# Attention beside a gated MLP: VectorE filler in measured portions, and the last output projection moved to the end

## The chip, the cores and the metric

The kernel runs on one core of a Trainium2 chip. The metric is the time of one execution on the device, in microseconds; the kernel before takes 751.76 us (median of three, 750.97 to 756.8). The engines of a core run side by side, each through its own queue of instructions in order, and meet through semaphores: TensorE (PE) multiplies matrices into PSUM, VectorE (DVE) adds and multiplies, ScalarE (ACT) copies and applies functions, GpSimd (POOL) and SyncE (SP) mostly start DMA transfers, as ScalarE can too.

## What is computed

```python
# A_x: 1 x 2048 x 1024 bf16; wqkv: 1024 x 3072; wo: 1024 x 1024
# w1, w3: 1024 x 3584; w2: 3584 x 1024
xn = layernorm(x)
qkv = (xn @ wqkv).reshape(B, S, 3, 32, 32)          # 32 heads of 32
idx = pos[:, None] - (arange(8) * 2)[None, :]       # 8 keys back, every 2nd
logits = einsum(q, k[idx]) * 32 ** -0.5             # idx < 0 masked
s = (softmax(logits) @ v[idx]).reshape(B, S, 1024) @ wo
h = silu(xn @ w1) * (xn @ w3)
g = silu(h @ w2)
out = x + s * g
```

Every token attends to 8 tokens (itself, and 2, 4, ... 14 back). There is no matrix product in the scores or the values: they are elementwise products of q, k and v with shifted views, on VectorE.

## The kernel before

**Products.** Each matrix product is done in blocks of 2 x 2 with seven products instead of eight. The function `seven` does one: with `a`, `b` for the two operands' quarters, `s` and `t` for sums of quarters, it runs the products a11 b11, s1 t1, a12 b21, (the product left over from the block before), s2 t2, s4 b22, s3 t3 on TensorE, eight 128x512 matmuls each, 56 in all. Between them ScalarE copies partial results from one PSUM tile to another (`act_copy`, L158), and VectorE adds the final combinations (`e12`, `e22`). PSUM has four tiles of 128x1024 f32, so a late copy or addition holds up a later product. The sums of weights (s, t) are made on VectorE, in the first half of the tokens, written out to `s_dram` and `t_dram`, and read back for the second.

**Stages.** Tokens fall in two halves b = 0, 1 of 1024, and attention in four chunks c = 0 to 3 of 512. The order of the matmuls is: layer norm and transposes, then six sevens for q, k and v (to about 170 us); `mlp_up(0)`, 14 blocks `fb` of 256 columns of w1 and w3 (170 to 350); `mlp_down(0)` (350 to 438); `wo(0)` (438 to 462); `mlp_up(1)` (462 to 637.5); `wo(1)` (637.5 to 664); `mlp_down(1)`, whose results `gated` multiplies with the attention output of `wo(1)` and adds to x (664 to the end).

**In a block of `mlp_up`** VectorE makes four sums of weights for the next block (`w_sums`, L547 to L550, 128x1024), the additions `um` (L581) and `h_sb` (L594) from PSUM and the product of the gate (L603, 128x2048). Every second block it also makes four sums of w2 (`w2_step`, L618 to L621, 128x1024). Their loads come through SyncE's queue into a ring of nine slots (`wring`, `r4`, `release`); a slot that is written out to DRAM can take a new load only when the write has landed.

**Attention as filler.** `scores` (L405 to L408: one product 128x4096 for each of 8 shifts, then three adds that halve), `score_sums` (sums over a head's 32 dimensions, on TensorE), `softmax` (L423 to L437) and `values` (L444 to L457) are VectorE work that fills the spaces between the sums. They are emitted in steps (`att_step`) with a low priority `BG`, at a few places of the stages, and the scheduler sets them into VectorE's order where it expects room; `behind(key)` keeps an instruction behind another on the same engine. `fetch_k` and `fetch_v` bring the next chunk through GpSimd's queue.

**`park`** gives a tile `pk` for a part of q, k or v that goes to DRAM, and a function `fin` that issues its write, on ScalarE's queue, together with one write of `spill` (the operands of the second half).

Of the kernel before, what the change touches and what calls it, by code (L numbers as in the profile page):

```python
# [17 lines left out]
def kernel(  # L18
# [161 lines left out]
    def seven(key, A, B, e11, e12, e22, e21, snap=None):  # L180
# [21 lines left out]
        act_copy(su2[:], pb[:])  # L202
        for i in I:
            mm(pe[:, i], s4[i], b22, False)
# [3 lines left out]
        e22(pb, sp5)  # L208

# [119 lines left out]
    def park(t, c, j0, name):  # L329
        tl = k4(name, (2, CH), BF16)  # L330
        dst = (q_dram, k_dram, v_dram)[t][c, :, j0:j0 + 2, :]

        def fin():
            m = nc.scalar.dma_start(out=dst, in_=tl[:])
            if spill:
                d, f = spill.pop(0)
                with tc.issue_after(m.ins):
                    nc.scalar.dma_start(out=d, in_=f)

        return tl[:], fin  # L340
# [6 lines left out]
    def qkv_copy(t, c, j0):  # L347
        def f(ps, *a):
            d, fin = qkv_dst(t, c, j0)
            with hp():  # L350
                if a:
                    nc.vector.tensor_add(d, ps[:], a[0][:])
                else:
                    anchor["c", t, c, j0] = nc.scalar.copy(out=d, in_=ps[:])  # L354
                fin()
        return f
# [29 lines left out]

    def fetch_k(c):
        if c == 0:
            return
        nc.gpsimd.tensor_copy(out=kT[:, :, 0:HALO], in_=kT[:, :, CH:CH + HALO])  # L390
# [4 lines left out]
    def fetch_v(c):  # L395
        nc.gpsimd.tensor_copy(out=vT[:, :, 0:HALO], in_=vT[:, :, CH:CH + HALO])
        nc.gpsimd.dma_start(out=vT[:, :, HALO:], in_=v_dram[c])

    def scores(c):
        q = qt[c]  # L400
        E = att_tile((W, CH), BF16, f"Es{c}")
        for w in range(W):
            o = HALO - DIL * w
            p_t = att_tile((NJ, CH), BF16, f"pt{c}_{w}")
            nc.vector.tensor_mul(p_t[:], q[:], kT[:, :, o:o + CH])  # L405
            nc.vector.tensor_add(p_t[:, 0:4, :], p_t[:, 0:4, :], p_t[:, 4:8, :])  # L406
            nc.vector.tensor_add(p_t[:, 0:2, :], p_t[:, 0:2, :], p_t[:, 2:4, :])
            nc.vector.tensor_add(E[:, w, :], p_t[:, 0, :], p_t[:, 1, :])  # L408
        sc[c] = E

    def score_sums(c):
        E = sc[c]
        zp = bank2(f"zp{c}")
        for h in range(2):
            for sq in range(4):
                nc.tensor.matmul(
                    zp[sq * 32:(sq + 1) * 32, h].rearrange("p (w t) -> p w t", t=P), lhsT=ones4[:],
                    rhs=E[:, h * 4:(h + 1) * 4, sq * P:(sq + 1) * P], start=True, stop=True,
                )
        sc[c] = E[:].bitcast(FP32).rearrange("p w n -> p (w n)").rearrange("p (a w t) -> p a w t", a=2, t=P)  # L420
        nc.scalar.copy(out=sc[c][:, 0], in_=zp[:].rearrange("p h (w t) -> p (h w) t", t=P))

    def softmax(c):  # L423
        Z = sc[c]
        z, zm, zs = Z[:, 0], Z[:, 1, 0:4], Z[:, 1, 4:8]
# [4 lines left out]
        nc.scalar.activation(out=z, in_=z, func=ACTF.Exp, scale=scale)  # L430
# [8 lines left out]
    def values(c, pairs=(0, 2, 4, 6)):  # L439
        E = pr[c]  # L440

        def pvmul(dst, w):
            o = HALO - DIL * w
            nc.vector.tensor_mul(dst, E[:, w, :].unsqueeze(1).to_broadcast([P, NJ, CH]), vT[:, :, o:o + CH])  # L444

        A = oT[:, c % 2]
        for w0 in pairs:
            B = att_tile((NJ, CH), BF16, f"B{c}_{w0}")
            if w0 == 0:
                pvmul(A, 0)  # L450
                pvmul(B[:], 1)
            else:
                C = att_tile((NJ, CH), BF16, f"C{c}_{w0}")
                pvmul(B[:], w0)
                pvmul(C[:], w0 + 1)
                nc.vector.tensor_add(B[:], B[:], C[:])
            nc.vector.tensor_add(A, A, B[:])  # L457

    def att_steps():
        with priority(BG - 10000):  # L460
            scores(0)
        yield
        score_sums(0)
        fetch_k(1)
        with priority(BG):
            softmax(0)
            scores(1)
            values(0)
            fetch_v(1)
        yield  # L470
        with priority(BG + 9000):
            fetch_k(2)
        yield
        score_sums(1)
        with priority(BG + 10000):
            softmax(1)
            scores(2)
            values(1)
            fetch_k(3)
            fetch_v(2)  # L480
        yield
        score_sums(2)
        with priority(BG + 20000):
            softmax(2)
        yield
        with priority(BG + 30000), behind("wo"):
            scores(3)
            values(2, (0, 2, 4))
        yield
        score_sums(3)  # L490
        with priority(BG + 40000):
            softmax(3)
            values(2, (6,))
            fetch_v(3)
            values(3)
        yield

    att_it = att_steps()

    def att_step():  # L500
        next(att_it)
# [17 lines left out]
    def up_load(b, fb):  # L519
# [7 lines left out]
        else:  # L527
            up_sums(b, fb, w1t, w3t)
            sa, s4 = tiles[b, fb][2:]
            nc.sync.dma_start(out=sa[:], in_=s_dram[fb, :, 0:2])  # L530
            nc.sync.dma_start(out=s4[:], in_=s_dram[fb, :, 3])
# [3 lines left out]
    def up_sums(b, fb, w1t, w3t):  # L535
        sa = r4(("sa", fb), (2, KH, 2 * P), FP16)
        half.append(half.pop(0))
        s4 = slot(5, (KH, 2 * P), FP16, half[0] * SLOT // 2)
        tiles[b, fb] = w1t, w3t, sa, s4

    def w_sums(fb):
        up_sums(0, fb, *tiles[0, fb])
# [3 lines left out]
        with behind(("m", fb - 1)):  # L546
            nc.vector.tensor_add(sa[:, 0], a21, a22)  # L547
            nc.vector.tensor_sub(sa[:, 1], sa[:, 0], a11)
            nc.vector.tensor_sub(s4[:], a12, sa[:, 1])
            nc.vector.tensor_sub(s3, a11, a21)  # L550
# [11 lines left out]
    def mlp_up(b, steps={}):  # L562
        order = [*range(b * FB // 2, FB - 1), *range(b * FB // 2), FB - 1]
        for n, fb in enumerate(order):
            steps.get(n, lambda: None)()
            if n == 0:
                up_load(b, fb)
                if b == 0:
                    w_sums(fb)
                up_load(b, order[1])  # L570
# [8 lines left out]
            def e12(pe, su2):  # L579
# [5 lines left out]
                if b == 0:  # L585
                    anchor["m", fb] = m
                    if fb + 1 < FB:
                        w_sums(fb + 1)
                if n + 2 < FB:
                    up_load(b, order[n + 2])  # L590

            def e22(pb, sp5):
                with hp():
                    m = nc.vector.tensor_add(h_sb[:, f2, CH:], pb[:], sp5[:])  # L594
                if b == 0:
                    anchor["t", fb] = m
                    w2_step(fb)

            def e21(pb, f2=f2, hl=hl, n=n, fb=fb):
                release(("w3", fb))  # L600
                with hp():
                    nc.scalar.copy(out=hl["g"][:, :, 0:CH], in_=pb[:])  # L602
                    nc.vector.tensor_mul(h_sb[:, f2, :], h_sb[:, f2, :], hl["g"][:])  # L603

            seven(f"m{b}_{fb}", up_A(b, fb), B0, e11, e12, e22, e21)

    def w2_step(fb):
        if fb % 2 == 0:
            tiles["t"] = [r4("t", (2, 2, CH)) for x in range(2)]
            for x in range(2):  # L610
                nc.sync.dma_start(out=tiles["t"][x][:], in_=w2_q[:, fb:fb + 2, x])
            return
        q = tiles["t"]
        q16 = [t[:].bitcast(FP16) for t in q]
        b11, b12, b21, b22 = [q[x][:, :, y] for x in range(2) for y in range(2)]
        o1, o3, o4, o2 = [q16[x][:, :, y] for x in range(2) for y in range(2)]
        with behind(("t", fb)):
            nc.vector.tensor_sub(o1, b12, b11)  # L618
            nc.vector.tensor_sub(o3, b22, b12)
            nc.vector.tensor_sub(o2, b22, o1)  # L620
            nc.vector.tensor_sub(o4, b21, o2)  # L621
        for x in range(2):
            nc.gpsimd.dma_start(out=t_dram[:, fb - 1:fb + 1, 2 * x:2 * x + 2], in_=q16[x])
        release("t")
# [13 lines left out]
    def mlp_down(b, done=lambda *a: None, mid=lambda n: None):  # L638
        NQ = (0, 4, 8, 11, 14)

        def rhs_tiles(kind, fh=0, dh=0, t=0):
            key = kind, fh, dh, t
            ops = [key]
            for f0, f1 in zip(NQ, NQ[1:]):
                wt = r4(key, (f1 - f0, CH), FP16 if kind == "t" else BF16)
                if kind == "t":
                    nc.sync.dma_start(out=wt[:], in_=t_dram[:, f0:f1, t, :])
# [23 lines left out]
        def sums(gp):  # L671
# [3 lines left out]
            with hp():  # L675
                for g in G2:
                    nc.vector.tensor_add(s1[g], a21[g], a22[g])
                for g in G2:
                    nc.vector.tensor_sub(s3[g], a11[g], a21[g])

# [5 lines left out]
        for gp in G2:  # L686
            act_copy(pb[gp][:], pa[gp][:])
            with hp():
                nc.vector.tensor_sub(s2[gp], s1[gp], a11[gp])
        rhs = rhs_tiles("w", 1, 0)  # L690
        product(pa, lst(a12), rhs, False)
        rhs = rhs_tiles("t", t=T2)
        for gp in G2:
            with hp():
                nc.vector.tensor_sub(s4[gp], a12[gp], s2[gp])
# [5 lines left out]

        product(pb, lst(s2), rhs, False, snap2)
        mid(0)
        for gp in G2:
            with hp():
                silu(g_tile(b, 0, 0, gp), pa[gp][:])
            done(0, 0, gp)
        rhs = rhs_tiles("t", t=T3)
        product(pb, lst(s3), rhs, False)
# [267 lines left out]
```

## Time and profile before

The profile shows one execution of 754.6 us span at a mean TensorE clock of 0.991.

| stretch, us | TensorE busy | VectorE busy | ScalarE busy | DMA share |
|---|---|---|---|---|
| 47 to 170 (qkv) | 116.1 of 123 | 103.2 | 51.3 | 0.63 |
| 170 to 350 (mlp_up 0) | 175.3 of 180 | 177.8 | 90.6 | 0.83 |
| 350 to 438 (mlp_down 0) | 85.7 of 88 | 73.5 | 18.7 | 0.75 |
| 438 to 462 (wo 0) | 24.0 of 24 | 15.3 | 10.1 | 0.85 |
| 462 to 637.5 (mlp_up 1) | 171.6 of 175.5 | 161.9 | 87.7 | 0.52 |
| 637.5 to 664 (wo 1) | 25.6 of 26.5 | 17.3 | 11.2 | 0.56 |
| 664 to 754 (mlp_down 1, end) | 85.2 of 90 | 28.6 | 15.3 | 0.37 |

An engine's busy time is the sum of its instructions' durations in a stretch. TensorE's is modelled, so the distance from one matmul's start to the next says more than its busy share: with no wait it is 0.2158 us for 128x512. In a list of waits a line reads: who waited, for whom, us in total, how often, the longest. In a timeline a line has the start, the duration and, in brackets, the idle time before and what ended it; ACTq and SPq are the queues that issue DMAs.

### The profile page before, as it was taken

What the parts mean: (1) busy time and instruction counts of PE and PEld (TensorE: products, weight loads), DVE (VectorE), ACT (ScalarE), POOL (GpSimd) and SP (SyncE); (2) the same over time, 40 slices, a digit from 0 to 9 for tenths busy, and PEclk for the clock granted to TensorE, in tenths of its full rate; (3) what the DMA queues carried; (4) which work ended last, traced back from release to release, by engine and by line L of the source; (5) the groups of instructions that cost most, each with busy time, mean ns of one, the idle gap of its engine ahead of it and who ended that gap; (6) DMA issues with size and microseconds to landing.
All of it is one profiled execution on the core that took longest, in us unless ns stands there. A gap on an engine that the chain in (4) does not pass through costs nothing.

```text
span 754.6 us, 8791 instructions
## 1 busy us (share of the span) xinstructions
PE 726.5 (96%) x3367; PEld 346.4 (46%) x3367; DVE 619.8 (82%) x602; ACT 312.9 (41%) x327; POOL 95.1 (13%) x156
## 2 busy tenths in 40 slices
PE   8999999889999999999899999999999999999997
PEld 4655555444444444434344444444444444444443
DVE  7997996789999999999899558999984999552143
ACT  5744344435444555443021443443565454420121
POOL 0000001320211253411001402000022000000000
PEclk9999999999999999999999999999999999999999
DMA  8366358844778899979575978554367543624631
GB/s 324 122 153 197 125 168 294 271 146 166 230 244 258 274 320 303 308 243 330 190 229 182 354 228 282 163 162 129 121 183 235 152 132 120 209 83 140 207 115 56
DMA packets 130218, 153.68 MB, mean 204 GB/s; under 512 B 14976, under 2 KB 100480, under 8 KB 129536
## 3 DMA queue, kind: packets, MB, share of 16 engines
q1 hardware_dynamic: 112960, 102.25, 44.0%
q0 software_dynamic: 11024, 37.76, 14.8%
q10 hardware_dynamic: 6192, 13.11, 4.7%
q8 instruction: 26, 0.43, 0.2%
q14 instruction: 16, 0.13, 0.1%
HBM read 107.48 MB, written 39.32 MB: 195 GB/s over the span
## 4 chain that ended last, share of the span: by engine, by line
DVE 44%; PE 36%; issue 12%; DMA 5%; ACT 1%; POOL 0%; SPq 0%; DVEq 0%; ACTq 0%; POOLq 0%
PE bq L148 5%; DVE pt L405 5%; PE db L148 5%; PE da L148 5%; PE bm L148 4%; DVE B L444 3%; PE de L148 3%; DVE oT L457 3%; DVE um L581 3%; PE am L148 3%; DVE h_sb L594 3%; PE aq L148 3%; DVE pt L406 3%; PE eq L148 3%; PE em L148 3%
## 5 line engine op out<-in xcount | busy, mean ns | idle before, releaser
L148 PEld LDWEIGHTS <-wring 128*128 128x128 f16 (+1 forms) x1952 | 205.1, 105 | 232.1 <-issue 19.8
L148 PE MATMUL bm<-xs,wring 128*128 128x512 f16 x672 | 156.5, 380 | 7.1 <-DVE h_sb L594 7.0
L148 PEld LDWEIGHTS <-h_sb 128*128 128x128 f16 (+1 forms) x976 | 103.0, 106 | 121.7 <-issue 12.7
L148 PE MATMUL am<-xT,wring 128*128 128x512 bf16 x448 | 107.3, 382 | 2.3 <-ACT bm L158 2.3
L405 DVE TENSOR_TENSOR pt<-qt,kT 128x4096 bf16<-128x4096 bf16 x32 | 73.1, 2287 | 1.0 <-ACT kT L354 0.4
L148 PE MATMUL db<-wring,h_sb 128*128 128x512 f16 x336 | 73.3, 379 | 0.0
L583 ACT ACTIVATE g<-um 128x1024 bf16<-128x1024 f32 x28 | 29.6, 1057 | 86.4 <-DVE um L581 82.1
L437 POOL DMA_DIRECT2D Ep<-pb x64 | 37.0, 586 | 128.2 <-DVE pb L433 120.7
L148 PE MATMUL em<-xs,wring 128*128 128x512 f16 x224 | 52.9, 379 | 0.0
L148 PE MATMUL da<-wring,h_sb 128*128 128x512 bf16 x224 | 50.7, 388 | 2.3 <-DMA wring<-in_B_w_dram 2.3
L148 PE MATMUL em<-xT,wring 128*128 128x512 bf16 x224 | 52.9, 379 | 0.0
L603 DVE TENSOR_TENSOR h_sb<-h_sb,g 128x2048 bf16<-128x2048 bf16 x28 | 34.1, 1217 | 8.0 <-ACT g L602 8.0
L406 DVE TENSOR_TENSOR pt<-pt 128x2048 bf16<-128x2048 bf16 x32 | 38.9, 1219 | 0.4
L577 ACT ACTIVATE h_sb<-am 128x1024 bf16<-128x1024 f32 x28 | 28.7, 1024 | 21.5 <-PE am L148 21.5
L158 ACT COPY pm<-em 128x1024 f32<-128x1024 f32 x28 | 28.3, 1011 | 21.1 <-PE em L148 21.1
L581 DVE TENSOR_TENSOR um<-em,um 128x1024 f32<-128x1024 f32 x28 | 34.0, 1216 | 3.2 <-PE em L148 3.2
L158 ACT COPY um<-bm 128x1024 f32<-128x1024 f32 x28 | 28.4, 1014 | 19.9 <-PE bm L148 19.9
L457 DVE TENSOR_TENSOR oT<-oT,B 128x4096 bf16<-128x4096 bf16 x16 | 36.5, 2283 | 0.1
L444 DVE TENSOR_TENSOR B<-Ep,vT 128x4096 bf16<-128x4096 bf16 x16 | 36.4, 2282 | 0.0
L602 ACT CAST g<-bm 128x1024 bf16<-128x1024 f32 x28 | 28.3, 1012 | 16.1 <-PE bm L148 15.8
L594 DVE TENSOR_TENSOR h_sb<-bm,pm 128x1024 bf16<-128x1024 f32 x28 | 34.0, 1214 | 0.4 <-PE bm L148 0.4
L158 ACT COPY bm<-am 128x1024 f32<-128x1024 f32 x28 | 28.0, 1002 | 10.1 <-PE am L148 10.0
(180 smaller groups left out, 886.5 us busy)
## 6 DMA issues: line engine op xcount, KB each, us to landing
wring<-in_B_w_dram SPq DMA_DIRECT2D x68, 512.0 KB, 5.6
wring<-t_dram SPq DMA_DIRECT2D x16, 512.0 KB, 4.6
s_dram<-wring POOLq DMA_DIRECT2D x14, 512.0 KB, 3.7
s_dram<-wring POOLq DMA_DIRECT2D x28, 256.0 KB, 4.8
t_dram<-wring POOLq DMA_DIRECT2D x14, 512.0 KB, 6.9
wring<-s_dram SPq DMA_DIRECT2D x28, 256.0 KB, 3.1
wring<-s_dram SPq DMA_DIRECT2D x14, 512.0 KB, 3.9
wring<-in_A_wqkv_dram SPq DMA_DIRECT2D x6, 1024.0 KB, 7.5
```

The costliest lines, as they stand in the source:

```text
L148: nc.tensor.matmul(ps, lhsT=lhs[k], rhs=rhs[k], start=(first and k == 0), stop=(k == n - 1), skip_group_check=not first,)
L158: nc.scalar.copy(out=out_, in_=in_)
L405: nc.vector.tensor_mul(p_t[:], q[:], kT[:, :, o:o + CH])
L406: nc.vector.tensor_add(p_t[:, 0:4, :], p_t[:, 0:4, :], p_t[:, 4:8, :])
L437: nc.gpsimd.dma_start(out=pr[c][r:P:NR, :, sq * P:(sq + 1) * P], in_=pb[sq * 32:(sq + 1) * 32, :, :])
L444: nc.vector.tensor_mul(dst, E[:, w, :].unsqueeze(1).to_broadcast([P, NJ, CH]), vT[:, :, o:o + CH])
L457: nc.vector.tensor_add(A, A, B[:])
L577: nc.scalar.activation(out=h_sb[:, f2, 0:CH], in_=pa[:], func=ACTF.Silu)
L581: m = nc.vector.tensor_add(su2[:], pe[:], su2[:])
L583: nc.scalar.activation(out=hl["g"][:, :, CH:], in_=su2[:], func=ACTF.Silu)
L594: m = nc.vector.tensor_add(h_sb[:, f2, CH:], pb[:], sp5[:])
L603: nc.vector.tensor_mul(h_sb[:, f2, :], h_sb[:, f2, :], hl["g"][:])
```

## The change

The changed kernel does the same products and orders the work around them in another way:

- **Attention in portions.** `att_work` yields the duration that each VectorE instruction is taken to have. `bg(us)` emits so many microseconds of it at a time and puts them behind the last fixed VectorE instruction (`anchor["v"]`). The portions are 8 us for a qkv seven, 4.5 us for a block of `mlp_up(0)`, 9 us for one of `mlp_up(1)`, and 7 to 10 us for each of six products of `mlp_down`. A `STOP` ends a portion where the next step needs something from another engine. It is to keep attention from getting ahead of additions that TensorE waits for.
- **Values** go in half-head passes, 128x2048 instead of 128x4096, and v is fetched by halves; the scores keep one buffer `pt` for a chunk.
- **The writes of `park` and `spill`** are issued on SyncE's queue instead of ScalarE's.
- **Weight sums.** `w_sums` is emitted inside `seven`, ahead of the product s4 b22; w2's sums are made for every block (`w2_load`, `w2_sums`, four of 128x512) instead of for every two; weights are loaded three blocks ahead instead of two, and s4 in a load of its own.
- **`wo(1)`** comes after `mlp_down(1)`, at the very end. The gates are made first, and the projection's results are multiplied with them; the last quarter is multiplied straight from PSUM in halves of 512 columns. The rows of x for the residual are loaded per quarter.

```diff
-            m = nc.scalar.dma_start(out=dst, in_=tl[:])
+            m = nc.sync.dma_start(out=dst, in_=tl[:])
...
         act_copy(su2[:], pb[:])
+        mid()
         for i in I:
             mm(pe[:, i], s4[i], b22, False)
         e12(pe, su2)
         for i in I:
             mm(pb[:, i], s3[i], t3, False)
         e22(pb, sp5)
+        bg(pace["n"])
...
+    def bg(us):
+        if us <= 0:
+            return
+        state_p[0] = tc.cur_priority
+        pace["credit"] += us
+        with priority(BG), behind("v"):
+            while pace["credit"] > 0:
+                t = next(att_it)
+                if t is STOP:
+                    pace["credit"] = min(pace["credit"], 4)
+                    break
+                else:
+                    pace["credit"] -= t
...
-        with behind(("m", fb - 1)):
-            nc.vector.tensor_add(sa[:, 0], a21, a22)
+        nc.vector.tensor_add(sa[:, 0], a21, a22)
...
             def e21(pb, f2=f2, hl=hl, n=n, fb=fb):
                 release(("w3", fb))
                 with hp():
                     nc.scalar.copy(out=hl["g"][:, :, 0:CH], in_=pb[:])
                     nc.vector.tensor_mul(h_sb[:, f2, :], h_sb[:, f2, :], hl["g"][:])
+                if n + 3 < FB:
+                    up_load(b, order[n + 3])
+                if b == 0:
+                    w2_sums(fb - 1)
+                    w2_load(fb)
...
+    def w2_load(fb):
+        tiles["t", fb] = r4(("t", fb), (2, 2, CH))
+        nc.sync.dma_start(out=tiles["t", fb], in_=w2_q[:, fb])
+
+    def w2_sums(fb):
...
+        nc.vector.tensor_sub(o1, b12, b11)
+        nc.vector.tensor_sub(o3, b22, b12)
+        nc.vector.tensor_sub(o2, b22, o1)
+        nc.vector.tensor_sub(o4, b21, o2)
+        nc.gpsimd.dma_start(out=t_dram[:, fb].rearrange("p (x y) n -> p x y n", x=2), in_=q16)
+        release(("t", fb))
...
+            if b == 1 and (u, dh) == (1, 0):
+                for i in I:
+                    nc.vector.tensor_mul(g[:, i], ps[:, i], g[:, i])
+                    nc.vector.tensor_add(g[:, i], g[:, i], x2[:, gp, i])
+                    nc.sync.dma_start(out=out_rows(out_flat, b, u, dh, gp)[:, i], in_=g[:, i])
+                return
...
-    wo(0, finish0)
-    mlp_up(1, {0: att_step, 6: att_step})
-    wo_prepare(1)
-    wo(1, finish1)
-    residual()
-    mlp_down(1, gated)
+    pace["n"] = 4.5
+    mlp_up(0)
+    mlp_down(0, lambda: mid(0), (7, 10, 10, 9, 9, 9))
+    with behind("dl"):
+        nc.sync.dma_start(out=xT[:], in_=x_dram[:])
+        nc.sync.dma_start(out=xs[:], in_=xs_dram[:])
+    wo(0)
+    state.add("wo")
+    pace["n"] = 9
+    mlp_up(1)
+    mlp_down(1, lambda: mid(1), (7, 10, 10, 9, 9, 9))
+    wo(1)
```

## The prediction

> **What bounds the kernel now.** I read the page's busy shares first.
>
> ```profile
> PE 726.5 (96%) x3367; PEld 346.4 (46%) x3367; DVE 619.8 (82%) x602; ACT 312.9 (41%) x327; POOL 95.1 (13%) x156
> DVE  7997996789999999999899558999984999552143
> DMA  8366358844778899979575978554367543624631
> ```
>
> TensorE is the bound, but not every microsecond is matmul work. In undisturbed stretches of the time-ordered view eight 128x512 matmuls start every 1.7265 us, 0.2158 us each, so a block of 56 takes 12.09 us. The kernel has 3,271 such matmuls (705.9 us), plus about 4 us of transposes and 2.2 us of the small softmax sums: a floor of 712 us. The first matmul starts at 1.3 and the last ends at 749.2, so TensorE loses 35.9 us. Adding up every start-to-start distance above the pitch places them: 6.5 before 40 us, 0.8 at 67, 0.9 at 91, 7.5 at 140 to 164 (end of the qkv stage), 6.7 in the first mlp_up, 4.2 in the first mlp_down, 0.8 at the softmax sums, 7.0 in the second mlp_up, 1.0 in the second wo. The last output leaves 5.4 us after the last matmul.
>
> The waits of TensorE, then of ScalarE and of the SyncE queue, name the causes:
>
> ```profile
> PE bm L148 <- DVE h_sb L594: 7.0, 9, 1.6
> PE aq L148 <- ACT bq L158: 6.2, 3, 3.3
> PE am L148 <- ACT bm L158: 2.3, 6, 0.5
> PE da L148 <- DMA wring<-in_B_w_dram: 2.3, 1, 2.3
> ...
> ACT bq L158 <- DVE pk L352: 17.9, 4, 7.4
> ...
> SPq L523 <- DMA t_dram<-wring: 28.9, 5, 6.4
> ```
>
> In both mlp_up stages TensorE waits for VectorE: it is busy 161.9 of 175.5 us in the second (the table by stretches), and nearly idle at the very end (28.6 of 90 us). At the end of qkv TensorE waits for a ScalarE copy, and ScalarE's timeline shows why:
>
> ```profile
> 136.07 0.33 ACTq L334 DMA_DIRECT2D v_dram<-pk  x1
> 144.35 1.00 ACT L158 COPY bq<-aq 128x1024 f32<-128x1024 f32 x1 [7.40 <-DVE pk L352]
> ...
> 154.34 4.40 ACTq L334 DMA_DIRECT2D q_dram<-pk  x2
> 158.78 1.00 ACT L158 COPY bq<-aq 128x1024 f32<-128x1024 f32 x1 [6.99 <-DVE Es L408]
> ```
>
> The write of pk stands in ScalarE's queue, waits for a pk that VectorE adds late (it is in attention), and the PSUM copy behind it waits too.
>
> **What the Trainium skill says.** "TensorE: Matmul & The Clock Gate", "Wait — 56ns, not 53.3ns?": 215.7 ns between 512-column matmuls warm, 426.7 cold; the trace has 0.2158 and, for about 3 us after stalls of 2.3 us or more, 0.43 (1.5 us lost each at 160, 365 and 529). "VectorE: DVE Perf Modes", on the TRN2 errata: a fixed cost per instruction. The trace agrees: two 128x2048 at 1.217 us against one 128x4096 at 2.28 are 0.15 us dearer. "Perfetto Trace Analysis", "DMA Instruction — HWDGE": the sequencer waits for the semaphores before it goes on. So does the queue above. "DMA: Bandwidth & Descriptors", "Anatomy of one DMA": 2.0 us plus bytes at 436 GB/s, 3.2 us for 512 KB; the trace's undisturbed 512 KB writes land in 2.9 to 3.5 us, but the median weight load in 5.6.
>
> **The change part by part.** TensorE's instructions are the same. What stands ahead of what is taken from the changed program's order on each engine.
>
> *Writes of pk to SyncE's queue.* ScalarE's copies no longer stand behind them: of 7.5 us at the end of qkv I keep 1.0, since pk adds may still lag a 2.2 us score multiply; the 0.9 at 91 us (TensorE waiting for a pk add) goes. What now queues behind these writes is weight loads for mlp_up blocks at least one seven away. Gain 7.4.
>
> *Attention in portions.* Per mlp_up block VectorE has four 128x1024 sums (0.68 each), two additions from PSUM (1.217 each) and one 128x2048 multiply (1.217), then w2 sums and attention. I added durations over the 13 block intervals of the first mlp_up, with 0.08 us taken off where an instruction doesn't need the one just before: before 162.9 us, after 150.8, against 13 x 12.09 = 157.2 of matmuls. The sum over blocks was the bound and is no longer. In the second mlp_up, most blocks come to 12.1 to 12.8, with two light ones (9.2 and 3.4), where before two had over 14. An addition may start 2.9 us late (product ready at 10.36 us in a block, its PSUM copy wanted at about 14.5, less its 1.2), so an excess of 0.6 us per block is absorbed for four or five blocks. Loss there 7.0 to 1.0; gain 6.0. The half-head passes raise attention from 300 to 309 us in all, hidden by the same slack and by mlp_down(1), where VectorE is idle.
>
> *w2 sums per block.* 56 of 128x512 at 0.42 instead of 28 of 128x1024 at 0.68: 23.5 for 19.0 us, inside the 150.8. But this adds a wait. For blocks 4 to 8 the queue order is: load of w1 for a later block, then w2_load. That w1 takes the slot that the previous w2 sums have just been written out from, so it waits for this write to land, and w2_load stands behind it. On VectorE, the first three w2 sums stand ahead of the addition of the fifth product, and wait for that load; behind this addition ScalarE's Silu waits, and TensorE for the PSUM tile. The loop: addition 1.2 + last sum 0.4 + issue 0.2 + write landing + queue and w1 issue 0.5 + load landing + three sums 1.3. With 4.3 for the write (512 KB writes: 3.7 at the median, 2.9 undisturbed) and 5.5 for the load (5.6) it is 13.4 us against 12.09. At block 3 the load waits only for TensorE (5.2 us into the block), so the addition starts at 11.7 us; five turns at +1.3 bring it to 18.2, less the latest harmless start 13.26: 4.9 us. The ends: 2.9 and 3.9 give 11 us, no loss; 6.9 (the median write of t_dram before, issued in pairs) and 5.6 give 16.1, 5 x 4.0 - 1.6 = 18.4 us. From block 9 on, w2_load has a whole block more. Add 1.5 for loads issued 5.2 us into other blocks that land late, and 1.1 for small waits: the first mlp_up loses 7.5, before 6.7. Loss 0.8.
>
> *Other loads.* mlp_down(0) still has a w2 chunk queued behind a t_dram write that lands 9 to 12 us into the stage; it is wanted at 15.5 and lands at 14.6 to 17.7: 2.5 for 4.2. Prefetch three blocks ahead, s4 alone, and xT/xs reloaded behind the last sums' loads: nothing, since wo(0) hides the 10 to 15 us of the reload.
>
> *Last projection at the end.* The same 112 matmuls, moved; its weight loads and sums lie under mlp_down(1), where VectorE and the DMA (0.37 busy) are free: gain 0.7. The tail grows: eight VectorE instructions stand after the last matmul, three multiplies of 128x512 from PSUM at about 0.6 (half of the 1.217 for 128x1024), their adds at 0.34 and two 128x1024 adds at 0.6, about 4.0 us, then 3.1 to the end of the last write as now: 7.1 for 5.4. Loss 1.7.
>
> Sum: -7.4 - 6.0 + 0.8 - 1.7 - 0.7 + 1.7 = -13.3 us. From the median 751.8: **738.5 us**.
>
> **The rivals.** *The loop doesn't bite:* writes to t_dram are alone now, not in pairs, and land in 3.5; then the first mlp_up loses 2.5 and the time is 733.5. For it: undisturbed 512 KB writes. Against: DMA already busy 0.83 over that stage. *The loop takes the gain:* 16.1 us per turn, 18.4 lost for 4.9: 752.0. For it: t_dram writes at 6.9 and SyncE's queue waiting for them up to 6.4 us already. *A new bound, slower:* the loop holds through blocks 4 to 13, with DMA saturated (1.0 in slices of the first mlp_up): ten turns at +4.0 lose 38.4 for 4.9, 772. For it: three transfers of 7 to 8 us at a time around 340 us. Against: from block 9 the order no longer ties it.
>
> **How the numbers follow.** Forecast 0.45, loop doesn't bite 0.25, loop takes the gain 0.18, slower 0.12. A tenth of the time may lie below 730 (if mlp_down(0) loses nothing either), a tenth above 757. Faster by over 1% (under 744.2): both first cases, 0.70. Within 1%: 0.18. Slower: 0.12.
>
> **What would show it.** Right: no ScalarE gap over 3 us with a pk write ahead of it at 140 to 160; second mlp_up at 12.1 to 12.3 us per block; first-mlp_up blocks 4 to 8 at 12.5 to 13.5, with VectorE's first w2 sum waiting for the DMA of w2; nothing but VectorE in the last 4 us before the final write. Wrong: blocks over 14 us in the first mlp_up, TensorE waiting on VectorE in the second, or a weight load late behind a pk write at the start of mlp_up.

## Result: where the time went

The changed kernel takes 763.07 us (median of four runs, 762.03 to 764.68) beside 751.58 before: the ratio is 1.0139, 95% interval 1.009 to 1.0189. It is slower by 1.4%, where 738.5 was forecast.

The stages, from the first matmul of one to the first matmul of the next, in the two profiled executions:

| stage | before | after | difference | forecast |
|---|---|---|---|---|
| layer norm and qkv | 170.2 | 167.5 | -2.6 | -7.4 |
| mlp_up(0) | 176.5 | 184.6 | +8.0 | +0.8 |
| mlp_down(0) | 91.3 | 88.2 | -3.0 | -1.7 |
| wo(0) | 24.2 | 27.0 | +2.8 | 0 |
| mlp_up(1) | 175.4 | 175.0 | -0.4 | -6.0 |
| wo(1) + mlp_down(1) | 111.7 | 110.7 | -1.0 | -0.7 |
| last product to the end | 5.4 | 7.6 | +2.2 | +1.7 |
| sum | 754.6 | 760.6 | +6.0 | -13.3 |

The profiled execution of the kernel before took 756.3, near the upper end of its range, so that the spans differ by 6.0 and the medians by 11.5; the rest can't be placed in a stage. The first matmul of mlp_up(0) is not a clean border either: behind it stand 8 matmuls of the last qkv seven before, and 16 after. So 8 x 0.2158 = 1.7 us of the -2.6, and of the +8.0, are only the border. To the first matmul of wo(0) it is 437.9 us before and 440.3 after.

### The profile page after: what moved, and what is told of

Read it like the earlier page. It is cut to its first block, busy times and chain, and to the rows that moved or that the text cites. A ratio compares the mean times of both kernels' runs of the same rounds, so it can differ in the third digit from the quotient of the medians.

```text
span 760.6 us, 8868 instructions
## 1 busy us (share of the span) xinstructions
PE 729.7 (96%) x3313; PEld 348.4 (46%) x3367; DVE 632.8 (83%) x690; ACT 311.2 (41%) x323; POOL 96.4 (13%) x162
## 4 chain that ended last, share of the span: by engine, by line
PE 62%; DVE 21%; DMA 10%; issue 4%; ACT 2%; SPq 0%; DVEq 0%; POOL 0%; ACTq 0%; POOLq 0%
PE bm L148 11%; PE am L148 8%; PE db L148 8%; PE bq L148 7%; PE em L148 7%; PE de L148 6%; PE da L148 6%; DMA wring<-in_B_w_dram 5%; PE eq L148 3%; PE aq L148 3%; DVE pt L413 3%; DVE pt L415 2%; DMA wring<-in_A_wo_dram 2%; DVE um L628 2%; DMA t_dram<-wring 2%
## 5 line engine op out<-in xcount | busy, mean ns | idle before, releaser
L148 PE MATMUL am<-xT,wring 128*128 128x512 bf16 x441 | 109.7, 382 | 7.5 <-ACT bm L158 6.9
L466 DVE TENSOR_TENSOR BC<-Ep,vT 128x2048 bf16<-128x2048 bf16 x56 | 66.8, 1219 | 2.9 <-DMA Ep<-pb 2.6
L148 PE MATMUL em<-xT,wring 128*128 128x512 bf16 x202 | 51.8, 379 | 1.2
L148 PE MATMUL da<-wring,h_sb 128*128 128x512 bf16 x220 | 48.9, 379 | 0.7 <-DMA wring<-in_B_w_dram 0.5
L476 DVE TENSOR_TENSOR oT<-oT,BC 128x2048 bf16<-128x2048 bf16 x32 | 39.0, 1219 | 0.4
L158 ACT COPY pm<-em 128x1024 f32<-128x1024 f32 x28 | 28.3, 1012 | 11.3 <-PE em L148 11.1
```

What stands on the lines that cost most here:

```text
L148: nc.tensor.matmul(ps, lhsT=lhs[k], rhs=rhs[k], start=(first and k == 0), stop=(k == n - 1), skip_group_check=not first,)
L158: nc.scalar.copy(out=out_, in_=in_)
L476: nc.vector.tensor_add(A, A, B if w0 else C)
```

## The profile after

The busy shares and two rows of the slices:

```profile
PE 729.7 (96%) x3313; PEld 348.4 (46%) x3367; DVE 632.8 (83%) x690; ACT 311.2 (41%) x323; POOL 96.4 (13%) x162
DVE  8986899299996879995999389993999998999246
DMA  9387254947877867987655986554465365353614
```

VectorE is busy 13 us longer, of which the half-head passes were worked out at 9. Its row has holes now in the first mlp_up (slices 10 to 19, counted from 1), where before it read 9 throughout. The list of waits says what they are (who, for whom, us, times, longest):

```profile
ACT bq L158 <- DVE pk L354: 17.6, 3, 7.2
DVE wring L669 <- DMA wring<-in_B_w_dram: 17.5, 5, 7.1
...
PE am L148 <- ACT bm L158: 6.9, 4, 4.3
```

The second line is new: 10.3 us of it, in four waits, lie in the first mlp_up, where VectorE waited for no load before; the longest, 7.1, stands at the start of mlp_down(0). And SyncE's queue, which stood 28.9 us behind writes to `t_dram`, now stands twice as long:

```profile
SPq L572 <- DMA t_dram<-wring: 59.8, 9, 11.8
```

**A cost that no list of waits shows** is seen in TensorE's timeline. Before, the eight small matmuls `zp` of `score_sums` stand together and the next product begins 0.55 us after the first:

```profile
124.04 0.62 PE L416 MATMUL zp<-Es,ones 128*32 128x512 bf16 x8
124.59 0.44 PE L148 MATMUL aq<-h_sb,wring 128*128 128x512 bf16 x1
```

After, they alternate one by one with a product's matmuls:

```profile
141.36 0.39 PE L428 MATMUL zp<-Es,ones 128*32 128x512 bf16 x1
141.69 0.44 PE L148 MATMUL aq<-h_sb,wring 128*128 128x512 bf16 x1
...
142.74 0.39 PE L428 MATMUL zp<-Es,ones 128*32 128x512 bf16 x1 [0.30 <-issue]
143.06 0.44 PE L148 MATMUL aq<-h_sb,wring 128*128 128x512 bf16 x1
143.43 0.39 PE L428 MATMUL zp<-Es,ones 128*32 128x512 bf16 x1
...
146.51 0.44 PE L148 MATMUL aq<-h_sb,wring 128*128 128x512 bf16 x1
```

Read the starts: each step from one kind to the other takes 0.32 to 0.37 us, although TensorE waits for nothing (ahead of 142.74 the record of one product matmul is missing from the trace). From the first small matmul to the start of the eighth product matmul it is 4.81 to 5.15 us, where apart it would be 0.55 + 7 x 0.2158 = 2.06: 2.7 to 3.1 us lost, four times, about 11 us. The busy share counts it as work. The cause is in the edit: `fore()` gives the eight the priorities that count up from `state_p`, and the product emitted after them has the same numbers, so the scheduler takes one of each in turn.

**The loop of w2** is in the chain of waits of the first mlp_up:

```profile
224.19 3.27 PE bm L148 x16
227.47 6.74 DMA wring<-in_B_w_dram
...
234.30 0.44 DVE wring L669
...
235.57 1.23 DVE um L628
...
237.78 1.01 ACT bm L158
```

A t_dram write lands at 227.0; only then SyncE issues the w1 load in that slot and, behind it, the load of w2 at 227.47; VectorE is idle 5.37 us at the first w2 sum, `um` is late behind it, ScalarE's Silu waits for `um` with the copy `bm` behind it, and TensorE stands still for 4.45, the longest stall of the kernel. The matmuls after it start 0.43 us apart at first, which loses another 1.7.

**In qkv** the stalls at 140 to 164 are gone, but there are new ones, of 2.41 us at 66 and of 1.6 at 119. The timeline of all engines at 66:

```profile
48.99 8.77 SPq L287 DMA_TRANSPOSE h_sb<-wring  x4
...
57.85 0.53 SPq L371 DMA_DIRECT2D wring<-in_A_wqkv_dram  x1
58.47 0.93 SPq L336 DMA_DIRECT2D k_dram<-pk  x2
...
66.22 1.23 DVE L354 TENSOR_TENSOR pk<-eq,uq 128x1024 bf16<-128x1024 f32 x1 [1.24 <-PE eq L148]
...
67.54 1.00 ACT L158 COPY bq<-aq 128x1024 f32<-128x1024 f32 x1 [7.17 <-DVE pk L354]
...
68.58 3.08 PE L148 MATMUL aq<-h_sb 128*128 128x512 bf16 x8 [2.41 <-ACT bq L158]
```

The wait of `pk` is put down to `eq`, which had ended at 61. What ended at 66.1 is the write of an earlier pk, whose buffer the addition takes: issued at 58.47, behind four transposing loads and a weight load on SyncE's queue, and landed 7.63 us later. On ScalarE's queue before, the writes were issued at 54.67 and 56.34 and landed in 3.7 and 3.2. The transposes themselves were held up by a fetch of q for chunk 1 (1 MB on GpSimd's queue at 51.8; before at 116.7): two landed in 6.7 and 7.2 where the two ahead of it took 3.1 and 3.3. The last line shows eight matmuls in 3.08 instead of 1.73 after the stall.

## The experiments

Theory: four separate causes, the alternating sums, the w2 loop, the early fetch of q, and the reload of xT and xs ahead of weights of `wo(0)`. Rivals: the DMA traffic as a whole, or the portions of attention, whatever the order. Ratios are to the kernel before on the same chip.

### Sums together, and sums apart in the kernel before

```diff
 # score_sums, in the loop over sq: all eight get the same priority
-                    nc.tensor.matmul(
+                    tc.cur_priority = state_p[0]; nc.tensor.matmul(
```

> The changed kernel with the eight small matmuls of each chunk's softmax sums given one priority, so that they stand together on TensorE (two, one product matmul, then six) instead of alternating with the product's matmuls. Theory A (alternating breaks up what ran side by side: eight pairs took 5.15 us where eight product matmuls and a group of sums took 2.28): four chunks at about 2.5 us, 753 us, the stretches of the sums at 0.6 to 1.0 us. Theory B (the time went to VectorE's extra work and late additions, and the sums only fill time in which TensorE would wait anyway): within 2 us of 763, with new waits of TensorE for VectorE.

759.65 us, 1.0081 (1.005 to 1.0112). The timeline has them nearly together, 1.2 us to the next product with one matmul of it in between:

```profile
141.73 0.39 PE L428 MATMUL zp<-Es,ones 128*32 128x512 bf16 x2
142.06 0.44 PE L148 MATMUL aq<-h_sb,wring 128*128 128x512 bf16 x1
142.42 0.61 PE L428 MATMUL zp<-Es,ones 128*32 128x512 bf16 x6
```

mlp_up(1), with two chunks of sums, went from 175.0 to 171.0, and qkv, with one, from 167.5 to 165.3; but mlp_up(0), which has one too, grew from 184.6 to 189.9, with a new stall of 5.0 us at 327.

The converse in the kernel before sets the priority back after the eight, so that the product has the same numbers:

```diff
-        E = sc[c]
+        E = sc[c]; p0 = tc.cur_priority
...
-        nc.scalar.copy(out=sc[c][:, 0], in_=zp[:].rearrange("p h (w t) -> p (h w) t", t=P))
+        nc.scalar.copy(out=sc[c][:, 0], in_=zp[:].rearrange("p h (w t) -> p (h w) t", t=P)); tc.cur_priority = p0
```

> The kernel before with the priority set back after each chunk's sums, so that in two chunks all eight, in one four and in one none of the small matmuls alternate with product matmuls. Theory A (alternating costs 2 to 2.9 us per chunk of eight): 4 to 7 us slower than the kernel before. Theory B (they fill time in which TensorE waits): within 1.5 us of it.

761.63 us, 1.0124 (1.0095 to 1.0152), 8.5 above its kernel before where theory A said 4 to 7. Two chunks alternate in full (4.81 us each), one in part, one hardly. mlp_up(1), with one of the full ones, went from 175.4 to 179.2, mlp_up(0) from 176.5 to 182.3. So the kernel before becomes about as slow as the changed one by this edit alone, and by more than the alternation's own 2.7 or so per chunk; where the rest comes from was not followed. That alternation costs time is shown both ways; how much of it reaches the end of a kernel depends on the waits around it.

### q fetched late, and the writes of pk

```diff
 # fetch_k: q only after k, whose fetch waits for the scores
+        anchor["kf"] = nc.gpsimd.dma_start(out=kT[:, :, HALO:], in_=k_dram[c])
+        with behind("kf"): nc.gpsimd.dma_start(out=qt[c][:], in_=q_dram[c])
```

> The changed kernel with the fetch of the second chunk's q (1 MB, issued at 51.8 us) put behind the fetch of its k on GpSimd's queue; no other queue changes. Theory A (this fetch runs beside the transposing loads, the writes of pk and two weight loads, makes them land in 7 to 11 us instead of 3, and so the stall at 66 us): stall at 66 us at or below 0.9 us as before, no half clock after it, qkv shorter by 3 to 4 us, 759.5. Theory B (the writes of pk are late because they stand in SyncE's queue): the stall stays at 2.6 us, 763.

756.46 us, 1.0049 (1.0024 to 1.0074). The transposes land in 3.1 to 3.3, the pk write is issued at 56.34, and the addition comes 2.2 us earlier, now with the write named as what it waited for:

```profile
64.02 1.22 DVE L354 TENSOR_TENSOR pk<-eq,uq 128x1024 bf16<-128x1024 f32 x1 [1.65 <-DMA k_dram<-pk]
```

The stall of 2.41 is gone (0.55 is left at 69 us) and qkv takes 165.0. What the late fetch saved is the write's issue, 2.1 us earlier; the write itself still took 7.56, just behind a weight load on SyncE's queue. wo(0) fell to 24.2 as well.

Does SyncE's queue for the pk writes earn anything? First they went to ScalarE only within qkv's part of the program, with q fetched early:

```diff
-            m = nc.sync.dma_start(out=dst, in_=tl[:])
+            m = (nc.sync if pace["n"] else nc.scalar).dma_start(out=dst, in_=tl[:])
```

> The changed kernel with the first writes of pk (up to the portions' start) back on ScalarE's queue, the later ones on SyncE's. Theory A (the early writes stand behind the transposing loads in SyncE's queue, land 4 us later, hold the pk buffers, and so VectorE's addition, ScalarE's copy and TensorE: 2.6 us and 1.7 at half clock at 66 us): 759.5 us. Theory B (the stall at 66 us comes from the transposes themselves, as before): 763.

768.46 us, 1.0186 (1.0141 to 1.0231); qkv 171.9. The fetch of q met transposes and pk writes alike (7.9 to 11.5 us for the last three transposes, 9.0 to 9.9 for the writes), so this run didn't separate the two. With q late, and all writes of `park` and `spill` back on ScalarE's queue (`nc.scalar` for `nc.sync` in both):

> The changed kernel with q fetched late and the writes of pk put back on ScalarE's queue; so against the run with q fetched late alone it undoes one part, the one from which the forecast took 7.4. Theory A (the part is worth what was forecast): the stalls at the end of the qkv stage are back (3.5 and 2.4 and half clock behind them), qkv 170 to 172 where the run with q late had 165, the time 760 to 764. Theory B (the stalls went with the portions of attention, or with the later fetch, not with the queue of the writes): qkv 165 to 166, the time 755 to 758.

760.15 us, 1.0102 (1.0044 to 1.0159), an interval that overlaps the one with q late alone. The two writes, now ahead of that weight load, landed in 4.0 and 3.3 us. qkv took 165.8 beside 165.0. ScalarE's queue still stands behind pk writes, 6.1 us at 135 and 2.8 at 155, where its timeline has the next copy right after the write, but TensorE's waits of the stage are short:

```profile
154.96 2.81 ACTq L336 DMA_DIRECT2D q_dram<-pk  x2
157.81 1.00 ACT L158 COPY bq<-aq 128x1024 f32<-128x1024 f32 x1 [5.90 <-PE eq L148]
```

```profile
PE aq L148 <- ACT bq L158: 3.2, 3, 1.4
```

So what ended the stalls at the end of qkv is mostly not the queue. The portions of attention, which would let VectorE add pk in time, are the likely reason, by what is left over; they were not taken out alone. The queue of the writes is worth 0.8 us of the stage; what it is worth to the whole time these runs leave open.

### The reload behind the weights of wo(0)

```diff
 # wo_prepare: the reload of xT and xs, which stands behind anchor "dl", comes after these
-            nc.sync.dma_start(out=wot[h, d][:], in_=wo_r[:, h * 4:(h + 1) * 4, d * CH:(d + 1) * CH])
+            anchor["dl"] = nc.sync.dma_start(out=wot[h, d][:], in_=wo_r[:, h * 4:(h + 1) * 4, d * CH:(d + 1) * CH])
```

> The changed kernel with the reload of xT and xs set behind the loads of wo's weights instead of ahead of three of them. Theory A (the 3.5 MB hold wo's weights until 439.7 us, its sums wait 10 us on VectorE, attention slips into the projection and its additions are late): wo(0) shorter by 2.5 us, 760.5 us. Theory B (the additions are late because the attention portion of the last product stands ahead of them in any case): 763, the wait for wo's weights shorter and the one of TensorE the same.

761.51 us, 1.0106 (1.0062 to 1.0151); wo(0) from 27.0 to 24.2, as in the kernel before. VectorE's wait for the weights, first after, then with the edit:

```profile
DVE h_sb L813 <- DMA wring<-in_A_wo_dram: 10.1, 1, 10.1
```

```profile
DVE h_sb L813 <- DMA wring<-in_A_wo_dram: 2.8, 1, 2.8
```

TensorE's 2.5 us of waits in wo(0) for additions of VectorE (L866) are gone. The way from the one wait to the other is not shown: with q fetched late wo(0) takes 24.2 too, while VectorE still waits 7.0 us for the weights and 13.4 us of attention stand in the stage (13.5 in the changed kernel). The intervals of the two ratios overlap, so a gain in the whole time isn't shown either; mlp_up(0) took 187.0.

### The w2 loop

Three edits to open it. The load of w2 ahead of the weight loads of the block:

> The changed kernel with w2's load and sums emitted ahead of the load of w1 and w3 for a later block, so that w2 gets slots of its own by turns and no load of it stands behind a weight load that waits for the write to t_dram. Theory A (the loop through SyncE's queue costs the first mlp_up 4.5 + 1.6 + 1.8 + 0.9 us): 754 to 755 us, first mlp_up shorter by 8 us, no wait of VectorE's first w2 sum above 2 us. Theory B (the DMA engines are full there and the loads would be late in any order): 761 to 763, the same waits at other places.

770.48 us, 1.0219 (1.0179 to 1.0259); mlp_up(0) 195.6. VectorE's waits at L669 in this stage rose from 10.3 to 17.1 us: the edit didn't remove what it was to remove. Two slots for w2, loaded half a block earlier (`w2_load` in `e12`), the sums behind the second addition (`w2_sums` in `e22`), weights still three blocks ahead:

> The changed kernel with w2's load issued after the fifth product's addition, half a block earlier, and its four sums put behind the addition of the sixth product of the next block, so that neither addition stands behind a w2 sum and a load has a whole block to land. Theory A (the wait of VectorE's first w2 sum, ahead of the addition that TensorE needs, cost the first mlp_up 8 us): first mlp_up at 175 to 178 us for 184.6, 754 us. Theory B (DMA full: weight loads are late in any order, as the second run of this series could be read): above 182 us, TensorE waiting for a weight tile or VectorE for w1 and w3 instead.

779.5 us, 1.0343 (1.0316 to 1.037); mlp_up(0) 195.9, mlp_down(0) 94.2. The wait moved: VectorE stood 16.5 us at the first of the weight sums (L596). With three more edits (sums, q, reload):

> The sums together, w2's sums behind the sixth product's addition, the reload behind wo's weights and the late fetch of q, all in one. Theory A (four separate causes): qkv 161.5 to 163, first mlp_up 173 to 176, wo(0) 24.2, second mlp_up 171, 740 to 743 us, faster than both kernels. Theory B (waits that replace each other): above 750.

765.59 us, 1.017 (1.014 to 1.02): qkv 162.0, wo(0) 24.2, mlp_up(1) 171.0, but mlp_up(0) 193.0. Without the w2 edit:

> The changed kernel with three edits at once: the eight softmax-sum matmuls of a chunk together, the early fetch of q behind the fetch of k, the reload of xT and xs behind the weights of wo(0). The loop of the w2 transposes in the first mlp_up is left as the change has it. Theory A (the three causes are separate and their prices add): qkv 162, wo(0) 24.2, the second mlp_up 171.0, the first still 184 to 190; the time 748 to 752, that is 0.5% either side of the kernel before. Theory B (what they give comes back as waits of the first mlp_up, which sets its own pace): the first mlp_up over 192 and the time 755 to 760.

756.77 us, 1.0055 (1.0037 to 1.0073). qkv 162.1, wo(0) 24.2 and mlp_up(1) 171.0 came out as their causes say, together 12.2 us; but mlp_up(0) took 193.4, 8.8 longer, as theory B had it. In 2.8 of the 8.8 TensorE waits for the last qkv products, behind the border. The chain of waits there shows the loop once more, at the end of the stage and through a w3 load for `w_sums`:

```profile
303.45 6.68 DMA t_dram<-wring
...
310.67 11.12 DMA wring<-in_B_w_dram
...
321.91 0.12 DVE wring L596
...
327.13 1.22 DVE h_sb L645
...
329.29 1.15 DVE um L628
...
331.42 1.01 ACT bm L158
```

To the first matmul of wo(0), no run is below the 437.9 us of the kernel before: 441.5 with the sums together, 438.7 with q late, 441.8 with the three edits, for 440.3 in the changed kernel. What the sums give up to there comes back as waits, and q's part does so beside them; what reaches the end of the run with three edits is the 4.0 us in mlp_up(1) and the 2.8 in wo(0).

Then the edit that also loads weights two blocks ahead and lets w2 and weight sums alternate behind the second addition:

```diff
 # e12, b == 0
+                    w2_load(fb)
+                    if n + 2 < FB: up_load(b, order[n + 2])
 # e22, b == 0
+                    with behind("v"): w2_sums(fb - 1)
 # mid
-                    w_sums(fb + 1)
+                    with behind("v"): w_sums(fb + 1)
```

> As the run with three edits, and in the first mlp_up the loop is opened: the w2 block is loaded in the first half of its own block, ahead of the weights of the next-but-one, and its additions stand on VectorE behind the second product of the next block and alternate with the additions of the coming weights, so that no addition on w2 stands ahead of an addition TensorE waits for. Theory A (the loop, load of w2 - addition - write - load of the next weights, is what lengthened the first mlp_up by 8): the first mlp_up 172 to 177, the time 735 to 742, about 2% below the kernel before. Theory B (the DMA traffic of the stage is the limit, and any order of it lands late): the first mlp_up over 184, its waits on VectorE again over 20 us at the loads of weights, the time 748 or more.

754.24 us, 1.0022 (1.0007 to 1.0037), the best of all, and still not below the kernel before. mlp_up(0) 183.6, but mlp_down(0) 91.9 instead of 86.3: a w2 chunk waits for a late t_dram write. And qkv takes 166.5 instead of 162.1: there a weight sum for mlp_up, whose load landed after 10.4 us among writes of pk, stands ahead of a pk addition on VectorE, and TensorE waits for that:

```profile
145.62 0.69 DVE L596 TENSOR_TENSOR wring<-wring 128x1024 f16<-128x1024 bf16 x1 [6.46 <-DMA wring<-in_B_w_dram]
146.23 1.22 DVE L354 TENSOR_TENSOR pk<-bq,pq 128x1024 bf16<-128x1024 f32 x1
...
147.50 2.51 PE L148 MATMUL bq<-h_sb,wring 128*128 128x512 f16 x8 [2.55 <-DVE pk L354]
```

The profiled span is what it was without the edit (755.4 beside 755.3). Alone:

> The changed kernel with the edit of the w2 loop alone. Theory A (the loop costs the first mlp_up 8 to 12 beside what sums and early q fetch cost in other stages): the first mlp_up 176 to 181 (its two chunks of sums, alternating, keep 4), the other stages as in the changed kernel, the time 751 to 757. Theory B (DMA traffic is the limit): the first mlp_up 184 or more, the time 760 or more.

765.42 us, 1.0162 (1.0114 to 1.0209): mlp_up(0) 179.6, mlp_down(0) 94.4. What one stage gained the next gave back.

### Parts of the old order put back

If the change's own w2 order made mlp_up(0) longer, the old order must shorten it. With `w2_step` (pairs, 128x1024) and loads two blocks ahead:

> The changed kernel with the w2 part of the first mlp_up put back as before: w2 loaded and transposed in pairs of blocks, 28 additions of 128x1024 behind the second addition from PSUM, weights loaded two blocks ahead. Theory A (the w2 part cost the stage its 8): the first mlp_up 174 to 178, the time 752 to 757. Theory B (the portions of attention and their DMA traffic cost it): the first mlp_up still 183 or more, the time 761 or more.

779.05 us, 1.0351 (1.0321 to 1.0382), mlp_up(0) 198.4. With `w_sums` emitted behind `um` too, which was to give loads and sums the order of before:

```diff
 # e12, b == 0
+                    anchor["m", fb] = m
+                    if fb + 1 < FB:
+                        with behind(("m", fb - 1)):
+                            w_sums(fb + 1)
```

> The changed kernel with the whole order of the first mlp_up as before: w2 in pairs, weights two blocks ahead, and the additions on the next block's weights behind the addition of the fifth product instead of ahead of it. Theory A (the order of loads and additions of the stage is what the change lost there): the first mlp_up 174 to 179, the time 751 to 758. Theory B (the portions of attention and the traffic around them lengthen it whatever the order): 184 or more, the time 761 or more.

779.08 us, 1.0336 (1.0318 to 1.0355), mlp_up(0) 196.1. VectorE's waits in the stage, in the kernel before and here:

```profile
DVE Es L380 <- ACT Es L430: 1.6, 1, 1.6
```

```profile
DVE wring L596 <- DMA wring<-in_B_w_dram: 28.1, 7, 7.1
```

No wait for a load before, 28.1 us here. But the order isn't that of before. There `behind(("m", fb - 1))` stands inside `w_sums`, where `fb` is the coming block, so that the sums follow `um` of the block at work. Here it stands at the caller, where `fb` is the block at work, and the sums follow `um` of the block ahead of it: one addition too early. In the kernel before, `um` of block 3 comes first, then the first sum for block 4:

```profile
220.33 1.21 DVE L581 TENSOR_TENSOR um<-em,um 128x1024 f32<-128x1024 f32 x1
...
222.59 0.68 DVE L547 TENSOR_TENSOR wring<-wring 128x1024 f16<-128x1024 bf16 x1
```

Here the sum for block 4 waits for its load, and `um` of block 3 stands behind it:

```profile
218.77 0.69 DVE L596 TENSOR_TENSOR wring<-wring 128x1024 f16<-128x1024 bf16 x1 [5.57 <-DMA wring<-in_B_w_dram]
...
224.51 1.22 DVE L628 TENSOR_TENSOR um<-em,um 128x1024 f32<-128x1024 f32 x1
```

From block 3 on, the weights had landed 7.7 us before the first sum at the median before, and only 0.1 us here. The loads themselves were no slower: SyncE's weight loads took 6.1 us at the median before and 5.8 here. So the waits go with sums that stand earlier behind loads two blocks ahead, and the run doesn't tell what attention does to them. Together with the three edits, with two and with three blocks ahead, and `w_sums` in `mid` or behind `um` of the block ahead:

> The same with the three other edits (sums together, q fetched late, the reload behind the weights of wo(0)). Theory A (all causes are separate): qkv 162, the first mlp_up 172 to 177, wo(0) 24.2, the second mlp_up 171; the time 737 to 744, that is 1 to 2% below the kernel before. Theory B (the first mlp_up takes back what the stages around it gain): the first mlp_up 184 to 193, the time 748 or more.

> As the run before, with the weights of the first mlp_up loaded three blocks ahead, as the change has it. Theory A (the pairs matter, not the prefetch): within 2 of the run before. Theory B (a load three blocks ahead takes a slot that is just written out, and the load of w2 stands behind it): the first mlp_up 4 or more longer than in the run before.

> The same with the sums together, q fetched late and the reload behind the weights of wo(0). Theory A: the first mlp_up 174 to 179, the time 739 to 747, below the kernel before. Theory B: the first mlp_up 184 or more, the time 748 or more.

> As the run before, but with the loads three blocks ahead as in the change; so against the run with pairs and prefetch of three it moves the weight sums alone. Theory A (the sums ahead of the addition cost the stage): the first mlp_up 5 or more below the 187.1 of that run. Theory B (they do not): 185 to 189.

| pairs of w2 and three edits | time | ratio (interval) | mlp_up(0) |
|---|---|---|---|
| two ahead, `w_sums` in `mid` | 766.38 | 1.0195 (1.0154 to 1.0235) | 193.9 |
| three ahead, `w_sums` in `mid` | 756.21 | 1.0056 (1.004 to 1.0072) | 187.1 |
| two ahead, `w_sums` behind the earlier `um` | 769.76 | 1.0215 (1.0185 to 1.0244) | 196.6 |
| three ahead, `w_sums` behind the earlier `um` | 756.53 | 1.0037 (1.0013 to 1.0061) | 185.9 |

Between these two places of the weight sums the intervals overlap, and in neither do all sums stand behind `um` as they did before. The loads three blocks ahead, which are also issued later in a block (`e21` for `e12`), make the stage 7 to 11 us shorter, where one theory said no difference and the other a longer stage. With them, pairs take the same time as w2 block by block (1.0056 beside 1.0055), so the split of w2's sums isn't what lengthened the stage.

What did so, beyond the wait for w2 in the trace and the alternation, stays open. The portions of attention, the weight sums ahead of `um`, and a traffic that no run looked at are all left: the stage holds 70.1 us of attention on VectorE for 86.4 before, but the transfers that spread the softmax weights (`Ep`) of two chunks, 32 for 16. Portions of another size, attention in its old order beside the other parts of the change, and all weight sums behind `um` as before were not tried.

## Why the prediction was wrong

**"TensorE's instructions are the same" failed, and it is the largest term that was put at nothing.** They are the same instructions in another order, and the order of the small sums costs 2.7 to 3.1 us a chunk by the trace, about 11 of the 19.3 us between the forecast -13.3 and the profiled +6.0. The text said that it took from the changed program's order on each engine what stands ahead of what; on TensorE it was not read. With the sums together qkv and mlp_up(1) gave 2.2 and 4.0 us back, and mlp_up(0) took 5.3.

**Writes of pk, "Gain 7.4".** The stalls it named went, but mostly not for its reason: with the writes back on ScalarE's queue qkv is only 0.8 longer. And "what now queues behind these writes" was half the question. The other half is what stands ahead of them: transposing loads and weight loads, so that a write landed at 66.1, and with the early fetch of q, which the forecast doesn't have, made the stall at 66 us. The stage gained 2.6; with q late 5.2, with the sums together as well 8.1; 1.7 of each is the border.

**Second mlp_up, "gain 6.0"**: right in its mechanism. With the sums together the stage is 171.0, 4.4 below before; the two chunks that alternate there took 4.0 of it back.

**First mlp_up, "Loss 0.8"**: the loop was named with its links (write landing, w1 issue, w2 load, sums, addition, Silu, PSUM), and it is in the trace. Its size was off. With the border taken out the stage lost 13.7 us beside its matmuls at 0.2158 (7.3 before), 2.8 of them by the alternation: about 10.9 for the 7.5 of the forecast. It didn't come in five turns of +1.3. The turn in the chain above alone cost 4.45 + 1.7: it has a w2 load at 6.74 for an assumed 5.5 and a write at 7.04 for 4.3, beyond the dear end of its range (5.6 and 6.9). (The cheap end of that range adds up to 10.4 us, not 11; there is no loss in either.) The forecast took VectorE's sum of durations over blocks, 150.8 of 157.2, for room; the trace has 10.3 us of waits for w2 in it. Why every edit to the loop brought new waits at other places stays open.

**mlp_down(0), "2.5 for 4.2"**: gain 3.0 for 1.7. **"Nothing, since wo(0) hides"** the reload: wrong, 2.8. It asked what the reload's own reader waits for, and not which loads stand behind it in the queue, the weights of wo(0); behind them it gave the 2.8 back, but so did the late fetch of q. **wo(1) at the end**, 0.7: 1.0 measured. **The tail**, "7.1 for 5.4": 7.6. The last lines of VectorE's timeline have the multiplications and additions it counted, at 0.6 and 0.37 each:

```profile
755.75 1.28 DVE L882 TENSOR_TENSOR h_sb<-wb,h_sb 128x512 bf16<-128x512 f32 x2
756.95 0.75 DVE L883 TENSOR_TENSOR h_sb<-h_sb,xw 128x512 bf16<-128x512 bf16 x2
```

Of the rivals, *the loop takes the gain* (752.0) was nearest in kind, without the sums; the slower one (772, DMA saturated through the stage) has the DMA at 0.79 there against it, less than the 0.83 before.

## What to carry to other kernels

Compare the order of every engine's queue, TensorE's too: ties in priority can interleave two groups of matmuls, at a cost that is booked as busy time and stands in no list of waits. When a transfer changes its queue, ask what stands ahead of it there and who waits for it to land, as well as what comes behind. On an engine that works in order, keep what waits for a load from standing ahead of what another engine waits for: here one sum of w2, 5.37 us late, stopped TensorE for 4.45.

## What the runs showed of the hardware

- A matmul with 32 columns of weights between two with 128: 0.32 to 0.37 us from start to start either way, against 0.2158 among full ones and 0.55 for eight small ones in a row.
- Landing times under other traffic: a write of pk 7.6 us for 3.2 to 3.7, a t_dram write of 512 KB 7.0, a w3 load 11.1, a transposing load 7.2 for 3.2 beside a 1 MB fetch, and 11.5 in one run.
- After the stall of 2.41 us at 66 us, eight matmuls took 3.08 us instead of 1.73; after one of 3.32 at 145 us in the kernel before, the next eight took 1.72. So the length of the stall alone doesn't decide it.
